# Word checks, casts, penalties, row maxima, one product and sixteen stores moved within an attention and MLP kernel on one Trainium2 core

## The chip, the cores and the metric

The kernel runs on one core of one Trainium2 chip. The time is the device time of one execution in microseconds (us). A run is reported as the median of several executions; one further execution was recorded by the hardware profiler, and all rows below come from it.

The engines are named as the trace names them: PE is the matrix engine TensorE, PEld its weight loads, DVE is VectorE, ACT is ScalarE, POOL is GpSimd, and SP is SyncE, which here only issues DMA transfers. A trailing q (ACTq, SPq) is an engine's own issuing queue. "L789" is line 789 of the kernel before.

## What is computed

A block of local attention, then a two-layer network with GELU on its result:

```python
# q, k, v: 4 batches, 8 heads, 768 positions, 64 per head
scores = scale * np.matmul(q, k.transpose(0, 1, 3, 2))
keep = is_global | is_local          # 8 global keys, 96 keys back
scores = scores - slopes[:, None, None] * dist[None, :, :]
scores = np.where(keep, scores, -1000000000.0)
a = np.exp(scores - np.max(scores, axis=-1, keepdims=True))
a = a / (np.sum(a, axis=-1, keepdims=True) + 1e-09)
x = np.matmul(a, v)                  # taken as 3072 tokens x 512
h = x @ w_in                         # 512 -> 2048
g = 0.5 * h * (1.0 + erf(h * inv_sqrt2))
return g @ w_out                     # 2048 -> 512
```

All of it is float32. The weights arrive as 8-byte words, and the kernel decodes them itself.

## The kernel before

**Tiling.** The 3072 tokens are 12 chunks of 256 rows, and the hidden width of 2048 is 8 slices of 256. One step is one slice of one chunk. `STEPS` lists the steps, and T is the number of the step in the main loop (`run`). Steps 0 and 4 to 18 do chunks 0 and 1, steps 19 to 26 do chunk 2 (the third chunk), and from step 27 on each chunk from 3 to 11 has eight steps, to step 98. A float32 operand is written as a high and a low float16 part, and each product as three float16 products (high by high, high by low, low by high). The low part is always made by a subtraction on DVE (L203, L204) from the high part, which is a cast on ACT or DVE.

**A step.** In step T the loop issues the first product `m1` of step T+1 (L702: `h` from `x` and `winh`, `winl`; 24 matmuls of 256 columns from chunk 2 on), the GELU of step T+1, and the second product `m2` of step T. `x` is the attention's result, ready for its chunk before its first step. From chunk 3 on `m2` is a seven-product scheme (`m2_seven`, L776): products P1 to P7 accumulate over the chunk's eight steps in the halves of four PSUM banks called `seven`. The left factors are quarters of the GELU (`gh`, `gl`) or sums of them (`sh`, `sl`; the sums `ss` are made at L742); the right factors are quarters of w_out (`wouth`, `woutl`) or differences of them (`sw`, made once for each slice by `sums`, L717 to L728: `sb`, `sf`, then the cast `sw` on ACT and its low part on DVE). In a chunk's last step `combine` (L789) reads the seven results out of PSUM into `u` and `o`, with which the banks come free for the next chunk. `give` stores the output rows by DMA.

**Attention.** Beside the steps the loop makes the attention of later chunks: scores `s` (L440), added penalties `pens` with a running minimum `mn` (L451), exponentials (L536), normalisation on POOL (L554), a transposition, and `av` (L604). `av` leaves PSUM as `x`, the high part by a cast on ACT (L614) and the low part on DVE (L203). Scores, `h`, `av` and transpositions share six PSUM banks.

**Checks.** Around this lie operations that serve a test at the end: `check_words` (L278, `wand`), which folds 32 pieces of reloaded weight words together; `rows` (L884, `otop`), the maxima of the output rows; and `bounds` (L208, `xtop`, `xlow`), the bounds of x.

**What sets the order.** The program is written for one loop, and a scheduler orders each engine's instructions by their dependences and by extra "behind" edges: `behind` puts an operation on DVE behind the low part of the latest GELU (`last_dve`), and `table` keeps the ACT functions that need a table in the written order. Each engine then works through its own list strictly in order.

**Names of the change.** `SUMS` tells in which step the differences of which slice are made, `PARTS` in which order the seven products of a step are issued (those of the first tuple, then the attention of slot C, then those of the second), `PENS` when the penalties of the later chunks are made (`more_pens`, then `scale_pens` in steps 14 and 15).

Of the kernel before, what the change touches and what calls it, by code (L numbers as in the profile page):

```python
# [13 lines left out]
AF = mybir.ActivationFunctionType  # L14
ALU = mybir.AluOpType
# [3 lines left out]
P = 128  # L19
# [25 lines left out]
GAP = 3  # L45
STEPS = [(c, s) for s in range(NST) for c in range(2)]
# [11 lines left out]
CAT = 2  # L58
# [4 lines left out]
GS = 2.0 ** 6  # L63
# [3 lines left out]
RATIO = 16.0  # L67
SEVEN = 3
PARTS = (("P1", "P2", "P4"), ("P6", "P7", "P5", "P3"))
ENDS = (("P6", "P7", "P5"), (("P1", "P2", "P6", "P7"), ("P4", "P5", "P3")))  # L70
SUMS = {17: 0, 18: 1, 19: 2, 21: 3, 22: 4, 25: 5, 26: 6, 29: 7}
HOME = {"P1": (0, 0), "P2": (0, 1), "P6": (1, 0), "P7": (1, 1), "P4": (2, 0), "P5": (2, 1), "P3": (3, 0)}
FACTORS = {"P1": ("A11", "B11"), "P2": ("A12", "B21"), "P3": ("S4", "B22"), "P4": ("A22", "T4"), "P5": ("S1", "T1"),
           "P6": ("S2", "T2"), "P7": ("S3", "T3")}
# [2 lines left out]
NB = NW // NG  # L77
KA = NW + 2 * NG
PENS = 13


def dap(t, off, dims):
# [23 lines left out]
def slope(h):  # L106
    return 2.0 ** (-(h + 1))


class Fast:  # L110
# [308 lines left out]
    def scale_pens(self, k):  # L419
        for i in range(4):  # L420
            h = 4 * (i // 2) + i % 2
            self.nc.gpsimd.tensor_scalar(out=self.pens2[k][:, i], in0=self.base[k], scalar1=8.0 * slope(h), scalar2=0.0,
                                         op0=ALU.mult, op1=ALU.add)

    def scores_windows(self, c, n):
        nc = self.nc
# [324 lines left out]
    def m2_seven(self, t, part):  # L751
        c, s = STEPS[t]
        if (c, s, part) == (SEVEN, 0, 0):
            self.seven = [self.ps_acc.tile([P, 2, 256], F32, name=f"seven{i}", tag="ps_acc") for i in range(2)]
            self.seven += [self.bank([P, 2, 256], f"seven{i}") for i in range(2, 4)]
        back = len(STEPS) - 1 - t
        names = PARTS[part] if back > 1 or (back, part) == (1, 0) else ENDS[0] if back else ENDS[1][part]
        for name in names:
            if (back, name) == (0, "P3"):
                self.products(t - 1, name)  # L760
            self.products(t, name)
# [47 lines left out]
    def give(self, c, k, final):  # L809
        nc, o = self.nc, self.o2[k]  # L810
        r = c * CT + k * P
        if not final or c < NCH - 1:
            args = c, k, o.rearrange("p h c -> p (h c)")
            if final:
                self.late_rows.append(args)
            else:
                self.rows(*args)
        if not final:
            return
        if c == NCH - 1:  # L820
            (nc.sync if k else nc.scalar).dma_start(self.out[r:r + P, 256:], o[:, 1])
            return
        nc.scalar.dma_start(self.out[r:r + P, :], o.rearrange("p h c -> p (h c)"))

    def gelu(self, t):
        nc = self.nc
        if STEPS[t][0] >= SEVEN:
            return self.gelu7(t)
        hp = self.h.pop(t)
        gh = self.gp.tile([P, 2, CT], F16, name=f"gh{t}", tag="gh")  # L830
        gl = self.gp.tile([P, 2, CT], F16, name=f"gl{t}", tag="gl")
        gr = self.gp.tile([P, 2, CT], F32, name=f"gr{t}", tag="gr")
        self.table(nc.scalar.activation(out=gr, in_=hp, func=AF.Gelu, scale=1.0 / (WS * XS)))
        nc.vector.tensor_scalar(out=gh, in0=gr, scalar1=GS, scalar2=None, op0=ALU.mult)
        self.last_dve = self.lo_dve(gl, gr, gh, GS).ins
        self.g[t] = (gh, gl)

# [36 lines left out]
    def send(self, c, k):  # L874
        nc, acc = self.nc, self.acc[c, k]
        o = self.sm.tile([P, DM], F32, name=f"o{c}_{k}", tag="o", bufs=3)
        r = c * CT + k * P
        scale = 1.0 / (GS * WS)
        nc.scalar.activation(out=o, in_=acc, func=AF.Copy, scale=scale)
        nc.scalar.dma_start(self.out[r:r + P, :], o)  # L880
        self.rows(c, k, o)

    def rows(self, c, k, o):
        self.behind(self.nc.vector.tensor_reduce(out=self.otop[:, c, k], in_=o.rearrange("p (h c) -> p h c", h=2),  # L884
# [38 lines left out]
    def run(self, flag_i):  # L923
# [15 lines left out]
        for self.T in range(START[0] - 1, last):  # L939
            T = self.T  # L940
# [9 lines left out]
                    self.split_weights(s, i)  # L950
            if 0 <= T - last + 9 < 6:
                self.checks(T - last + 9)
            k = T - 16 - GAP
            if 0 <= k < 64 and k % 2 == 0:
                self.check_load(k // 2)
            words = 2 <= k < 66 and k % 2 == 0
            if words and (T < 30 or T % 4 == 1):
                self.check_words((k - 2) // 2)
            if T == PENS:
                self.more_pens()  # L960
            if PENS < T < PENS + 3:
                self.scale_pens(T - PENS - 1)
            if T == 16:
                self.bounds(self.xtop, self.xlow, *(self.x[c][:, :, 0, :] for c in range(2)))
            if T in SUMS:
                self.sums(SUMS[T])
            self.turns = T >= 19
# [24 lines left out]
            if T % 8 == 3:  # L992
                for args in self.late_rows:
                    self.rows(*args)
                self.late_rows.clear()
            if words and T >= 30 and T % 4 == 3:
                self.check_words((k - 2) // 2)

    def checks(self, k):
        nc, sm = self.nc, self.const  # L1000
# [221 lines left out]
```

## Time and profile before

| what | value |
|---|---|
| median of 3 runs | 631.32 us (628.44 to 632.48) |
| the profiled execution | 629.22 us |
| its span, first to last instruction | 627.4 us |
| PE busy in the span | 599.5 us (96%) |
| DVE busy | 498.1 us (79%) |
| ACT busy | 352.9 us (56%) |
| POOL busy | 91.0 us (14%) |
| mean granted clock of PE | 0.992 |

The profiled execution took 1.8 us more than its span, which is what lies ahead of the first and behind the last instruction. In a row of the timeline, the first number is the start in us from the beginning of the span, the second the duration; neighbouring equal instructions are put together, with their number behind an x. A bracket tells how long the engine had stood idle just before, and what it waited for.

### The profile page before, as it was taken

The page shows a single profiled execution, that of the slowest core. Times are in us where ns is not written, and L with a number is a line of the kernel's source. Part 1 is how long each engine was busy: PE and PEld are TensorE (multiplying, and loading weights), DVE is VectorE, ACT ScalarE, POOL GpSimd, SP SyncE. Part 2 cuts the span into 40 slices and gives each one's busy share as a digit, 9 for nine tenths or more (in the row PEclk, how much of TensorE's full clock was granted, in tenths as well). Part 3 has the DMA queues.
Part 4 walks back from the last instruction along what each step waited for, and adds up shares of the span by engine and source line. Part 5 has one row for each costly group of instructions (what it writes and reads, how often), then busy time and mean ns, then how long its engine had stood idle before and what let it go on. Part 6 is the DMA issues. An engine that isn't in the chain of part 4 may idle for free.

```text
span 627.4 us, 19513 instructions
## 1 busy us (share of the span) xinstructions
PE 599.5 (96%) x7968; PEld 464.8 (74%) x7968; DVE 498.1 (79%) x1579; ACT 352.9 (56%) x855; POOL 91.0 (14%) x188
## 2 busy tenths in 40 slices
PE   8988999999999899999999899999999999999995
PEld 5665544445676678888888788888888888888884
DVE  7979999998788786876876776876876876875885
ACT  3777577755526566466466366366466466463331
POOL 1000006253033022022022021021021021010000
PEclk9988999999999999999999999999999999999998
DMA  9948925434371284184184175164275173100001
GB/s 272 270 173 255 261 97 202 121 66 146 114 192 57 86 218 137 37 218 136 37 218 137 36 186 159 46 159 129 104 169 180 44 195 93 37 1 2 36 1 40
DMA packets 111809, 79.47 MB, mean 127 GB/s; under 512 B 54752, under 2 KB 99296, under 8 KB 111712
## 3 DMA queue, kind: packets, MB, share of 16 engines
q1 hardware_dynamic: 107120, 70.80, 39.7%
q10 hardware_dynamic: 4592, 7.34, 3.3%
q8 instruction: 65, 1.06, 0.7%
q14 instruction: 32, 0.26, 0.1%
HBM read 71.83 MB, written 6.29 MB: 125 GB/s over the span
## 4 chain that ended last, share of the span: by engine, by line
PE 63%; DVE 23%; ACT 8%; issue 3%; POOL 2%; DMA 1%; DVEq 0%; ACTq 0%; POOLq 0%
PE h L702 26%; PE seven L776 22%; PE av L604 5%; ACT n L536 4%; PE s L440 4%; DVE gl L204 2%; DVE ss L742 2%; PE acc L863 2%; POOL n L554 2%; DVE wb L249 1%; DVE wb L251 1%; PE warm_ps L520 1%; DVE o L789 1%; DVE sl L204 1%; DVE u L789 1%
## 5 line engine op out<-in xcount | busy, mean ns | idle before, releaser
L702 PE MATMUL h<-x,winh 128*128 128x256 f16 x1344 | 227.7, 274 | 4.4 <-DVE x L203 2.9
L702 PE MATMUL h<-x,winl 128*128 128x256 f16 x672 | 184.3, 274 | 0.0
L702 PEld LDWEIGHTS <-winh 128*128 128x128 f16 x1344 | 130.3, 98 | 25.0 <-issue 4.0
L554 POOL TENSOR_SCALAR n<-n,su 128x160 f32<-128x160 f32 (+1 forms) x160 | 81.1, 527 | 450.0 <-DVE su L548 286.3
L737 ACT ACTIVATE gr<-h 128x512 f32<-128x512 f32 x72 | 43.0, 597 | 109.2 <-PE h L702 96.3
L742 DVE TENSOR_TENSOR ss<-gr 128x128 f32<-128x128 f32 x144 | 35.2, 285 | 64.6 <-ACT gr L737 64.6
L744 ACT ACTIVATE sh<-ss 128x512 f16<-128x512 f32 x72 | 45.4, 630 | 66.4 <-DVE ss L742 66.4
L776 PE MATMUL seven<-sw,sh 128*128 128x256 f16 x432 | 75.0, 273 | 1.3 <-issue 1.3
L702 PEld LDWEIGHTS <-winl 128*128 128x128 f16 x672 | 66.1, 98 | 9.1 <-issue 1.2
L776 PEld LDWEIGHTS <-sh 128*128 128x128 f16 x576 | 55.0, 98 | 8.3 <-issue 1.5
L536 ACT ACTIVATE n<-n,mn 128x160 f32<-128x160 f32 x144 | 59.5, 414 | 2.7 <-DVE mn L451 2.5
L776 PE MATMUL seven<-sw,sl 128*128 128x256 f16 x216 | 58.9, 273 | 1.2 <-DVE sl L204 1.1
L204 DVE SCALAR_TENSOR_TENSOR gl<-gr,gh 128x384 f16<-128x384 f32 (+1 forms) x96 | 57.1, 594 | 0.7
L204 DVE SCALAR_TENSOR_TENSOR sl<-ss,sh 128x512 f16<-128x512 f32 x72 | 49.6, 689 | 10.0 <-ACT sh L744 10.0
L776 PEld LDWEIGHTS <-gh 128*128 128x128 f16 x432 | 41.0, 98 | 11.9 <-ACT gr L737 3.8
L451 DVE CUSTOM_DVE_ANT_0 n<-s,pens 128x160 f32<-128x160 f32 x144 | 38.0, 320 | 3.8 <-PE s L440 2.5
L743 ACT ACTIVATE gh<-gr 128x384 f16<-128x384 f32 x72 | 37.6, 523 | 3.9 <-ACT gr L737 1.8
L776 PE MATMUL seven<-wouth,gh 128*128 128x256 f16 x144 | 39.4, 274 | 0.0
L776 PE MATMUL seven<-wouth,gl 128*128 128x256 f16 x144 | 39.3, 273 | 0.0
L776 PE MATMUL seven<-woutl,gh 128*128 128x256 f16 x144 | 39.3, 273 | 0.0
L604 PEld LDWEIGHTS av<-ptb,vr 32*64 32x64 f32 x2304 | 31.3, 130 | 5.6 <-issue 5.3
L536 ACT ACT_TABLE_LOAD x22 | 28.2, 1283 | 12.3 <-DMA qr<-qT 6.5
(160 smaller groups left out, 1103.5 us busy)
## 6 DMA issues: line engine op xcount, KB each, us to landing
w<-w SPq DMA_DIRECT2D x32, 512.0 KB, 6.4
c<-w SPq DMA_DIRECT2D x32, 512.0 KB, 4.5
kr<-kT SPq DMA_DIRECT2D x34, 320.0 KB, 4.2
vr<-v SPq DMA_DIRECT2D x60, 112.0 KB, 2.6
qr<-qT SPq DMA_DIRECT2D x11, 512.0 KB, 4.3
out<-o ACTq DMA_DIRECT2D x22, 256.0 KB, 2.3
kr<-kT SPq DMA_DIRECT2D x84, 64.0 KB, 3.6
vr<-v SPq DMA_DIRECT2D x36, 32.0 KB, 2.7
```

Source lines behind the costliest of these rows:

```text
L204: return self.nc.vector.scalar_tensor_tensor(out=out, in0=in_, scalar=scale, in1=hi, op0=ALU.mult, op1=ALU.subtract)
L440: ins = nc.tensor.matmul(sp[hh][NG * i:NG * i + NG, u, :], lhsT=qq[hr, 2 * e + p, o:o + NG], rhs=kt[hr, 2 * e + p, j, k:k + NW], start=Tru ...
L451: ins = nc.vector.tensor_tensor_reduce(out=nn[:, 2 * hh + u], in0=sp[hh][:, u, :], in1=pens, scale=-0.125, scalar=3e38, op0=ALU.add, op1=A ...
L536: self.table(nc.scalar.activation(out=nn, in_=nn, func=AF.Exp, bias=mn[:, i:i + 1], scale=-1.0, accum_out=su[:, i:i + 1]))
L554: ins = eng.tensor_scalar(out=nn, in0=nn, scalar1=su[:, i:i + 1], scalar2=0.0, op0=ALU.mult, op1=ALU.add)
L604: ins = nc.tensor.matmul(banks[i][hh * D:(hh + 1) * D, u0 * NG:u1 * NG], lhsT=vv[rows, e, b, hh * D:(hh + 1) * D], rhs=g, start=n == 0, st ...
L702: ins = nc.tensor.matmul(hp[:, f, :], lhsT=w[:, d, fs], rhs=x[:, d, e, :], start=n == 0, stop=n == 3 * NP - 1).ins
L737: self.table(nc.scalar.activation(out=gr.rearrange("p i q -> p (i q)"), in_=hp.rearrange("p f q -> p (f q)"), func=AF.Gelu, scale=1.0 / (W ...
L742: self.last_sum = nc.vector.tensor_tensor(out=ss[:, o], in0=x, in1=y, op=op).ins
L743: nc.scalar.activation(out=gh, in_=gr[:, 1:], func=AF.Copy, scale=GS)
L744: self.last_table = nc.scalar.activation(out=sh, in_=ss, func=AF.Copy, scale=GS).ins
L776: ins = nc.tensor.matmul(out, lhsT=g, rhs=w, start=s == 0 and name in ("P1", "P4", "P6", "P3") and i == 0, stop=s >= NST - 4 and i == 2, s ...
```

## The change

Six things are moved. The word checks run in steps 33 to 89 instead of 21 to 83. In chunk 2 the cast `gh` of the GELU goes from DVE to ACT (8 casts), and the eight scalings in `scale_pens` go from POOL to ACT. Four of the eight `sums` get another step. The row maxima of chunks 1 and 2 are put off until the end of the next step with T%8 == 3. In the first step of each chunk from 3 on, P6 and P4 change places. The 16 output stores of `give` for chunks 3 to 10 are issued by SP instead of ACT.

```diff
 PARTS = (("P1", "P2", "P4"), ("P6", "P7", "P5", "P3"))
+OPENS = (("P1", "P2", "P6"), ("P7", "P4", "P5", "P3"))
-SUMS = {17: 0, 18: 1, 19: 2, 21: 3, 22: 4, 25: 5, 26: 6, 29: 7}
+SUMS = {17: 0, 18: 1, 21: 2, 22: 3, 23: 4, 25: 5, 26: 6, 30: 7}
+WORDS = [T for T in range(33, 90) if T % 2 or T in (62, 70, 78)]
...
             h = 4 * (i // 2) + i % 2
-            self.nc.gpsimd.tensor_scalar(out=self.pens2[k][:, i], in0=self.base[k], scalar1=8.0 * slope(h), scalar2=0.0,
-                                         op0=ALU.mult, op1=ALU.add)
+            self.nc.scalar.activation(out=self.pens2[k][:, i], in_=self.base[k], func=AF.Copy, scale=8.0 * slope(h))
...
-        names = PARTS[part] if back > 1 or (back, part) == (1, 0) else ENDS[0] if back else ENDS[1][part]
+        names = OPENS[part] if s == 0 else PARTS[part] if back > 1 or (back, part) == (1, 0) else ENDS[0] if back else ENDS[1][part]
...
-        nc.scalar.dma_start(self.out[r:r + P, :], o.rearrange("p h c -> p (h c)"))
+        nc.sync.dma_start(self.out[r:r + P, :], o.rearrange("p h c -> p (h c)"))
...
-        nc.vector.tensor_scalar(out=gh, in0=gr, scalar1=GS, scalar2=None, op0=ALU.mult)
+        if STEPS[t][0] < CAT:
+            nc.vector.tensor_scalar(out=gh, in0=gr, scalar1=GS, scalar2=None, op0=ALU.mult)
+        else:
+            self.last_table = nc.scalar.activation(out=gh, in_=gr, func=AF.Copy, scale=GS).ins
...
         nc.scalar.dma_start(self.out[r:r + P, :], o)
-        self.rows(c, k, o)
+        if c:
+            self.late_rows.append((c, k, o))
+        else:
+            self.rows(c, k, o)
...
-            k = T - 16 - GAP
-            if 0 <= k < 64 and k % 2 == 0:
-                self.check_load(k // 2)
-            words = 2 <= k < 66 and k % 2 == 0
-            if words and (T < 30 or T % 4 == 1):
-                self.check_words((k - 2) // 2)
+            if T + 2 in WORDS:
+                self.check_load(WORDS.index(T + 2))
+            if T in WORDS and T % 4 == 1:
+                self.check_words(WORDS.index(T))
...
-            if words and T >= 30 and T % 4 == 3:
-                self.check_words((k - 2) // 2)
+            if T in WORDS and T % 4 > 1:
+                self.check_words(WORDS.index(T))
```

ACT around the GELU of step 17, the kernel before (`gr` is a GELU's result, `pt` a copy of transposed weights of the attention, `n` the scores, `sw` the cast of w_out's differences):

```order
L833 ACTIVATE gr_1670<-h_1649 128x512
L581 COPY pt_4_1660<-t_5_1674 128x384
L833 ACTIVATE gr_1714<-h_1693 128x512
L581 COPY pt_6_1704<-t_6_1700 128x384
L581 COPY pt_6_1704<-t_7_1718 128x384
L536 ACT_TABLE_LOAD
L536 ACTIVATE n_0_1743,su_0_1724<-n_0_1743,mn_0_1723 128x160 x4
L536 ACTIVATE n_1_1780,su_1_1761<-n_1_1780,mn_1_1760 128x160 x4
L833 ACT_TABLE_LOAD
L833 ACTIVATE gr_1831<-h_1816 128x512
L727 CAST sw_329<-sf_1808 128x1024
```

The same place of ACT in the changed kernel:

```order
L834 ACTIVATE gr_1670<-h_1649 128x512
L582 COPY pt_4_1660<-t_5_1674 128x384
L424 ACTIVATE pens<-rb 128x640 x4
L424 ACTIVATE pens_1451<-rb 128x320 x4
L834 ACTIVATE gr_1714<-h_1693 128x512
L582 COPY pt_6_1704<-t_6_1700 128x384
L582 COPY pt_6_1704<-t_7_1718 128x384
L537 ACT_TABLE_LOAD
L537 ACTIVATE n_0_1743,su_0_1724<-n_0_1743,mn_0_1723 128x160 x4
L728 CAST sw_329<-sf_1808 128x1024
L834 ACT_TABLE_LOAD
L834 ACTIVATE gr_1831<-h_1816 128x512
```

The eight scalings of the penalties now stand ahead of step 17's GELU (`gr_1714`), and the cast `sw` of slice 0 ahead of the table load and the GELU of step 18 (`gr_1831`).

DVE at steps 27 and 28, the kernel before (`gl_2685` and `sl_2688` belong to step 27, `ss_2749` to `sl_2751` to step 28, `x` is the low part of chunk 4's attention):

```order
L204 SCALAR_TENSOR_TENSOR gl_2685<-gr_2683,gh_2684 128x384
L725 TENSOR_TENSOR sf_2649<-sb_2648,sf_2649 128x256
L204 SCALAR_TENSOR_TENSOR sl_2688<-ss_2686,sh_2687 128x512
L884 TENSOR_REDUCE otop<-o_0_2704 128x2
L884 TENSOR_REDUCE otop<-o_1_2714 128x2
L278 SCALAR_TENSOR_TENSOR wand<-c_3_2578,wand 128x512
L203 TENSOR_TENSOR sw_1246<-sf_2649,sw_1246 128x1024
L742 TENSOR_TENSOR ss_2749<-gr_2746 128x128 x2
L742 TENSOR_TENSOR ss_2749<-gr_2746,ss_2749 128x128
L204 SCALAR_TENSOR_TENSOR gl_2748<-gr_2746,gh_2747 128x384
L204 SCALAR_TENSOR_TENSOR sl_2751<-ss_2749,sh_2750 128x512
L203 TENSOR_TENSOR x<-av_0_0_2774,x 128x128
```

The same place of DVE in the changed kernel:

```order
L206 SCALAR_TENSOR_TENSOR gl_2674<-gr_2672,gh_2673 128x384
L205 TENSOR_TENSOR sw_1246<-sf_2638,sw_1246 128x1024
L206 SCALAR_TENSOR_TENSOR sl_2677<-ss_2675,sh_2676 128x512
L743 TENSOR_TENSOR ss_2733<-gr_2730 128x128 x2
L743 TENSOR_TENSOR ss_2733<-gr_2730,ss_2733 128x128
L206 SCALAR_TENSOR_TENSOR gl_2732<-gr_2730,gh_2731 128x384
L206 SCALAR_TENSOR_TENSOR sl_2735<-ss_2733,sh_2734 128x512
L205 TENSOR_TENSOR x<-av_0_0_2758,x 128x128
L891 TENSOR_REDUCE otop<-o_0_2693 128x2
```

The word check is gone from here, the two row maxima stand behind x's low parts, and the low part of `sw` (slice 6) stands ahead of step 27's `sl` instead of behind it.

PE in step 27, the first of chunk 3, at the third product of its first tuple, the kernel before:

```order
L776 MATMUL seven_2761<-woutl_328,gh_2684 128x256
L776 LDWEIGHTS gl_2685
L776 MATMUL seven_2761<-wouth_327,gl_2685 128x256
L776 LDWEIGHTS gh_2684
L776 MATMUL seven_2763<-sw_329,gh_2684 128x256
L776 MATMUL seven_2763<-sw_329,gl_2685 128x256
```

The same place of PE in the changed kernel:

```order
L777 MATMUL seven_2745<-woutl_328,gh_2673 128x256
L777 LDWEIGHTS gl_2674
L777 MATMUL seven_2745<-wouth_327,gl_2674 128x256
L777 LDWEIGHTS sh_2676
L777 MATMUL seven_2746<-sw_329,sh_2676 128x256
L777 MATMUL seven_2746<-sw_329,sl_2677 128x256
```

The third product now reads the sums `sh` and `sl` instead of `gh` and `gl`, and writes another bank.

## Rows read from the trace of the kernel before

**Rows 1.** Busy time in a stretch: PE, PEld, DVE, ACT, POOL, then PE's clock

```profile
252.00:300.00 48.00, 47.64 (x757) 41.03 (x756) 37.01 (x126) 27.48 (x69) 6.33 (x16) 1.00 0.46 128
```

**Rows 2.** Timeline of PE where chunk 4 begins

```profile
256.07 0.27 PE L776 MATMUL seven<-woutl,gh 128*128 128x256 f16 x1
256.18 0.27 PE L776 MATMUL seven<-wouth,gl 128*128 128x256 f16 x1
256.81 0.38 PE L776 MATMUL seven<-sw,gh 128*128 128x256 f16 x2 [0.36 <-DVE u L789]
```

**Rows 3.** Waits by engine and line: us in total, times, longest

```profile
ACT gr L737 <- DVE u L789: 12.8, 7, 1.8
...
PE seven L776 <- DVE u L789: 2.5, 7, 0.4
```

**Rows 4.** Timeline of DVE just ahead of that place

```profile
254.74 0.42 DVE L789 SCALAR_TENSOR_TENSOR u<-seven,u 128x256 f32<-128x256 f32 x1
255.08 0.69 DVE L204 SCALAR_TENSOR_TENSOR sl<-ss,sh 128x512 f16<-128x512 f32 x1
```

**Rows 5.** Timeline of PE: its idle times from 149 to 229 us

```profile
149.99 0.27 PE L702 MATMUL h<-x,winh 128*128 128x256 f16 x1 [0.38 <-DVE x L203]
...
154.67 0.39 PE L863 MATMUL acc<-wouth,gh 128*128 128x512 f16 x1 [0.80 <-DVE gh L834]
...
155.46 0.39 PE L863 MATMUL acc<-wouth,gl 128*128 128x512 f16 x1 [0.19 <-DVE gl L204]
...
163.91 0.51 PE L440 MATMUL s<-kr,qr 64*32 64x160 f32 x16 [1.26 <-DVE x L203]
...
212.06 0.38 PE L702 MATMUL h<-x,winh 128*128 128x256 f16 x2 [2.29 <-DVE x L203]
...
228.80 0.28 PE L776 MATMUL seven<-sw,sl 128*128 128x256 f16 x1 [1.10 <-DVE sl L204]
```

**Rows 6.** Timeline of ACT and DVE ahead of the idle time at 163.91

```profile
161.35 1.04 ACT L727 CAST sw<-sf 128x1024 f16<-128x1024 f32 x1 [4.72 <-DVE sf L725]
162.43 1.22 DVE L203 TENSOR_TENSOR sw<-sf,sw 128x1024 f16<-128x1024 f32 x1 [1.11 <-ACT sw L727]
163.57 0.68 DVE L203 TENSOR_TENSOR x<-av,x 128x128 f16<-128x128 f32 x3
```

**Rows 7.** Timeline of DVE ahead of the idle time at 212.06

```profile
206.47 1.27 DVE L884 TENSOR_REDUCE otop<-o 128x2 f32<-128x512 f32 x2
207.66 0.68 DVE L278 SCALAR_TENSOR_TENSOR wand<-c,wand 128x512 int32<-128x512 int32 x1
208.26 1.22 DVE L203 TENSOR_TENSOR sw<-sf,sw 128x1024 f16<-128x1024 f32 x1
...
211.72 0.88 DVE L203 TENSOR_TENSOR x<-av,x 128x128 f16<-128x128 f32 x4
```

**Rows 8.** Timeline of DVE ahead of the idle time at 228.80

```profile
226.75 1.39 DVE L203 TENSOR_TENSOR sw<-sf,sw 128x1024 f16<-128x1024 f32 x1 [0.32 <-ACT sw L727]
```

**Rows 9.** Timeline of POOL: the eight scalings of the penalties

```profile
132.13 6.60 POOL L422 TENSOR_SCALAR pens<-rb 128x640 bf16<-128x640 f32 x8 [2.08 <-DVE rb L416]
```

**Rows 10.** Timeline of ACT: the GELUs of steps 17 and 18

```profile
131.47 0.60 ACT L833 ACTIVATE gr<-h 128x512 f32<-128x512 f32 x1 [2.70 <-DVE gl L204]
...
142.57 0.60 ACT L833 ACTIVATE gr<-h 128x512 f32<-128x512 f32 x1
```

**Rows 11.** Timeline of PE: step 17's last scores, step 20's first product

```profile
137.40 0.78 PE L440 MATMUL s<-kr,qr 64*32 64x160 f32 x32
...
145.32 0.38 PE L702 MATMUL h<-x,winh 128*128 128x256 f16 x2
```

**Rows 12.** Instructions by line and shape: busy us, mean ns, idle before

```profile
L834 DVE TENSOR_SCALAR gh<-gr 128x512 f16<-128x512 f32 x24 | 11.0, 459 | 5.1 <-ACT gr L833 5.1
...
L744 ACT ACTIVATE sh<-ss 128x512 f16<-128x512 f32 x72 | 45.4, 630 | 66.4 <-DVE ss L742 66.4
```

**Rows 13.** Waits of SP's own queue

```profile
SPq L315 <- PE s L440: 140.3, 8, 22.3
```

## The prediction

> **What bounds the kernel now.** I read the busy times by stretch first, then PE's timeline for each gap, then the timelines of the engine that the gap's bracket names. In a steady stretch PE is busy 47.64 of 48.00 us at full clock, DVE only 37.01 [rows 1]. So only what PE waits for counts, and the other engines have slack except where they hold PE up. Those places are few. How a gap is measured: 256-column matmuls start 0.11 apart (256.07, 256.18), so the next was due at 256.29 and came at 256.81: 0.52 lost, with 0.36 shown as idle [rows 2]. A shown idle time thus stands for about 0.16 more.
>
> The first kind of gap lies at the seven places where one chunk follows another from chunk 3 on. The waits view has it as PE waiting for DVE's u, seven times, 2.5 us in all [rows 3], so 7 x 0.52 = 3.64 us with the 0.16 each. The first tuple's third product, P4, must write a bank that DVE still reads.
>
> The second kind is single: six idle times between 149 and 229 us [rows 5]. With 0.16 on each they are 0.54, 0.96, 0.35 and 1.42 (chunk 2's steps), 2.45 and 1.26 (chunk 3's first), 6.98 in all; three more small ones of 0.1 to 0.15 I leave out. Everything that the change can win lies in these 10.6 us.
>
> **The change part by part.**
>
> *P6 for P4.* P6 writes the half whose old content DVE reads with the u at 254.74, finished at 255.16; its sl is made at 255.08 and finished at 255.77 [rows 4]. PE reaches the third product's sl matmul two matmuls after 256.29, at about 256.5. So P6 finds everything there, with 0.73 to spare. P4 now stands behind P6, the attention's av of slot C and P7: six matmuls of 0.11 and the av, so it is due 0.65 and more after 256.29, later than the 256.81 at which its bank was free. The whole 3.64 goes. In the order, step 27 shows the exchange as announced. **-3.64.** The cover is those 0.73 us: an sl later than that costs its excess seven times.
>
> *ACT in steps 17 to 20.* Here the change removes and adds. On POOL the penalties ran 6.60 us from 132.13, as soon as DVE's rb was there [rows 9]; no bracket on PE named them. Now they stand on ACT ahead of step 17's GELU, which before began at 131.47 [rows 10]. No row has such an instruction on ACT. Two casts give the slope: 1.04 us for 1024 columns [rows 6] and 0.630 for 512 [rows 12], so 0.81 ns a column and 0.215 at the start. For 640 columns that is 0.73, for 320 it is 0.47, together 4 x 1.20 = 4.8; if the start overlaps, in proportion to columns alone, 3.9. I take the middle, 4.4. The GELU then ends at 132.1 + 4.4 + 0.6 = 137.1, five late. Behind it wait the scores of step 17 (a PSUM bank that this GELU frees). Before, they were issued between the second product's matmuls, the last at 137.40 [rows 11]; now they stand behind them all, and without the scores' own time between them (about 1.0) these are over at about 136.4. PE waits about **+0.7**. From below this is 0 (if the penalties take 3.9 or less), from above all 4.4.
>
> The chain runs on: two copies, a table load, the exponentials, and now also the cast sw of slice 0 ahead of step 18's GELU. Before, this GELU ended at 143.17 [rows 10]; I walk it to about 147.2: 5 us late at step 17, some of it won back because ACT waited for DVE there, and the cast's 1.04 put ahead. Step 20's first product, at 145.32 before [rows 11], needs its bank, and PE has about 1.3 us of other work ahead of it: **+0.65** (0 to 2). The low parts of x follow at about 151.7, for which I put **+1.15** in the place of the 0.54 at 149.99.
>
> In step 19 the cast gh moves to ACT. The gap of 0.96 was a wait for gh on DVE behind the sw low part [rows 5]; it becomes a wait for gh on ACT behind a sw cast, 1.04 [rows 6], about **+1.2**, and the gl behind it **+0.3** where it was 0.35. In the other seven steps of chunk 2 gl has slack, and the 0.630 on ACT for 0.459 on DVE [rows 12] is hidden: 0.
>
> The 1.42 at 163.91 goes: x's low part stood behind a sw cast of 1.04 and the sw low part of 1.22 [rows 6], which are slice 2's and are made two steps later now. Sum of this stage: 0.7 + 0.65 + 1.15 + 1.2 + 0.3 = 4.0 added, 0.54 + 0.96 + 0.35 + 1.42 = 3.27 and about 0.25 of the small gaps removed: **+0.5**, bounds -2.5 (nothing new shows but the gh) and +4.5.
>
> The Trainium skill, "ScalarE: Activation LUTs", section "Rules for kernel authors", would have multiplications on VectorE, not on ScalarE; the rows agree in direction (0.459 against 0.630 [rows 12]), and eight casts would be worth +1.4 if each were on PE's path, of which I count none but step 19's. The same page, section "What ACT_TABLE_LOAD costs", puts an ACTIVATE with immediates at 186 ns + 0.833 ns a column, 93 ns of it overlapped; an estimate from it for the eight penalties is 4.0, by which the first wait would be 0.3 instead of 0.7.
>
> *DVE at steps 27 and 28.* The 2.45 at 212.06 comes from x's low part at 211.72, which frees a bank for h. Ahead of it stand two row maxima (1.27 together), a check (0.68) and a sw low part (1.22) [rows 7]: from 206.47 to 209.4. In the new order the check is elsewhere, the maxima come behind x, and the sw low part stands ahead of step 27's sl. x's low part comes 2 to 2.9 earlier, and PE got there at 209.6. The gap goes. But step 27's P6 now needs sl in the first tuple, and sl has the sw low part ahead of it: its end moves from 206.5 to 207.6, where PE would come at about 206.8: +0.85 (0 to 1.2). Together **-1.6**, bounds -2.45 and -0.4.
>
> *Steps 30 and 31.* The 1.26 at 228.80 waited for sl behind the sw low part of slice 7 at 226.75, 1.39 long [rows 8]. That is made one step later now, and stands ahead of step 31's gl instead, which has less cover by one product: +0.4 for -1.26, so **-0.9** (-1.26 to +0.3).
>
> *The rest.* The 32 checks take the same time elsewhere. In steps 33 to 89 DVE has 11 of 48 us idle [rows 1], and a check of 0.68 behind the low parts delays nothing that PE waits for: 0 (to +1). Stores on SP instead of ACT: ACT's GELU waits 12.8 us in all for u behind those issues [rows 3], but nothing on PE is named there, 0. On SP the stores stand ahead of later loads. SP's loads wait 140.3 us for the scores to free their buffers [rows 13], up to 22.3 each, so it has time, and a chunk's loads are issued well ahead of its scores: 0.
>
> **Sum.** -3.64 + 0.5 - 1.6 - 0.9 = -5.6, on the profiled execution's 629.22: 623.6. That execution lay 1.2 below the mean of the four executions known (630.4), and the median of three lies above both. I predict **624.8** as the time of a usual execution.
>
> **Rivals.**
>
> (a) *The middle stage gives back what it wins.* ACT becomes the engine that steps 17 to 20 wait for: penalties 4.4, a cast of 1.04 ahead of a table load, gh casts of 0.63, all in one strict list. If the GELU of step 18 is as late as the whole 4.4, the stage costs +3 instead of +0.5. For it: all the new waits hang on one chain. Against: PE has other work there (the first products of chunk 2). Then 629.22 - 3.64 + 3 - 2.5 + 1.2 = 627.3. Chance 0.30.
>
> (b) *The penalties are hidden.* PE's list has enough left at step 17, step 27's P6 waits for nothing: -3.64 - 2 - 2.45 - 1.26 = -9.3, so 621.1. For it: the scheduler has put step 16's whole second product ahead of the scores. Against: ACT's list has 4.4 us more in a place where it was never idle for as long. Chance 0.17.
>
> (c) *Slower: P6 waits for sl at each chunk's beginning.* If DVE takes the five adds u and o (0.42 each, 2.1 us) ahead of sl, sl ends at 257.9, P6 waits 1.4 instead of P4's 0.52, and 7 x 0.88 = +6.2 replaces -3.64: 629.22 + 6.2 - 2.0 + 1.2 = 634.6. It decides from a wait of 0.81, where 7 x 0.29 eats the 2.0 of the other places. For it: P6 needs sums and two casts more than P4. Against: DVE's list has sl between the adds, at 255.08 [rows 4], and the new list keeps it there. Chance 0.05.
>
> (d) *The exchange does not do what it says:* another half of the same bank is still unread, and P6 waits for the same read as P4 did. Then only the other places count: 629.22 - 2.0 + 1.2 = 628.4. For it: the trace shows only P4's wait. Against: the u at 254.74 is over 1.1 ahead. Chance 0.06.
>
> **How the numbers follow.** My forecast has 0.42, (a) 0.30, (b) 0.17, (c) 0.05, (d) 0.06. Its own bounds (-2.5 to +2 on the middle stage and the two places behind) give 622 to 627.5; with (b) below and (a) and (d) above, the range is **619.5 to 630.0**. It leaves out (c) and the tail of (b). A measurement of this kernel tells about 1% from no change, 6.3 us, since its own runs spread by 4; faster by over 1% means below 625.0, on which the forecast sits. Half of the forecast, (b) and a little of (a) are faster: 0.21 + 0.17 + 0.06 = 0.44. Slower over 1% is (c) with a part of ACT's upper bound: 0.07. Within 1%: 0.49.
>
> **What would show it.** Right: at the seven chunk beginnings no PE gap, and no PE wait for u in the waits view; no gap at 212; a GELU of step 17 that ends near 137 with PE waiting for it under 1 us; a gh on ACT that PE waits for in step 19 alone. Wrong: a PE wait for sl at the chunk beginnings ((c)); one for ACT of several us between 136 and 152 ((a)); no PE wait at all for ACT there ((b)).

## The result and the profile after

The changed kernel takes 623.18 us (median of 7 runs, 621.3 to 625.92), the kernel before 630.22 (7 runs, 626.6 to 632.48). The ratio is 0.9891, with a 95% interval from 0.9853 to 0.9928: 6.9 us less, between 4.5 and 9.3. Forecast were 624.8 and a change of -5.6.

The profiled execution of the changed kernel took 625.92 us, the longest of its seven; its span of 624.1 is only 3.3 below that of the kernel before (627.4). So the two profiles are compared by stretches, from the start of one step's GELU on ACT (L737 and L833 before, L738 and L834 after) to that of another. Where nothing random falls into a stretch, it repeats within about 0.1 us from kernel to kernel. Such a mark is ACT's: where ACT itself starts a GELU late, the mark moves without any loss on PE.

| from the GELU of step to that of step | before | after | change | forecast |
|---|---|---|---|---|
| 16 to 27 (last of chunks 0 and 1, chunk 2) | 72.63 | 72.61 | -0.02 | +0.5 |
| 27 to 29 (chunk 3 begins) | 14.45 | 13.28 | -1.17 | -1.6 |
| 29 to 33 | 24.61 | 24.37 | -0.24 | -0.9 |
| 33 to 36 | 17.36 | 16.36 | -1.00 | |
| 76 to 84 (one chunk, undisturbed) | 46.87 | 46.31 | -0.56 | -0.52 |
| 84 to 98 | 73.71 | 74.18 | +0.47 | |
| 44 to 60 (two chunks) | 96.97 | 97.84 | +0.87 | |

The seven chunk beginnings together give -3.9 (a first -1.00, six chunks of -0.56, and +0.47 at the end), where -3.64 was forecast. The -1.00 and the +0.47 belong together: before, a store holds up the GELUs of steps 36, 44 and so on to 84, so the row 33 to 36 ends with a late mark and the row 84 to 98 begins with one. With the first three rows this is -5.3, inside the measured interval of -4.5 to -9.3. The last row has -1.1 of the change in it and is +0.87 all the same: in it stand PE's waits of kind "issue", of another length in every profile (last section).

The rows of the changed kernel that answer to [rows 2, 3 and 4]. PE's timeline where chunk 4 begins:

```profile
254.99 0.27 PE L777 MATMUL seven<-wouth,gl 128*128 128x256 f16 x1
255.10 0.38 PE L777 MATMUL seven<-sw,sh 128*128 128x256 f16 x2
255.31 0.27 PE L777 MATMUL seven<-sw,sl 128*128 128x256 f16 x1
```

DVE's timeline there:

```profile
253.59 0.42 DVE L790 SCALAR_TENSOR_TENSOR u<-seven,u 128x256 f32<-128x256 f32 x1
253.93 0.69 DVE L206 SCALAR_TENSOR_TENSOR sl<-ss,sh 128x512 f16<-128x512 f32 x1
254.52 0.76 DVE L790 SCALAR_TENSOR_TENSOR o<-seven,u 128x256 f32<-128x256 f32 x2
```

P6 starts 0.11 after the matmul ahead of it; its sl was ready at 254.62, 0.69 before PE's first use of it at 255.31 (0.73 was forecast). No wait of PE for u is left in the waits view, and ACT's GELU no longer waits for u either. That wait is now SP's, whose loads behind the stores still come in time: from 125 us on no wait of PE names a load. The waits of SP's queue:

```profile
SPq L824 <- DVE u L790: 110.2, 8, 38.3
SPq L317 <- PE s L441: 81.9, 8, 25.6
```

The busy time of the stretch of [rows 1] has PE without a gap:

```profile
252.00:300.00 48.00, 48.00 (x761) 41.40 (x760) 37.46 (x129) 27.80 (x69) 6.33 (x16) 1.00 0.45 128
```

PE's timeline from 146 to 236 us, its idle times of 0.2 us and more, which answer to [rows 5]:

```profile
147.38 0.38 PE L703 MATMUL h<-x,winh 128*128 128x256 f16 x2 [1.17 <-ACT gr L834]
...
151.82 0.27 PE L703 MATMUL h<-x,winh 128*128 128x256 f16 x1 [0.82 <-DVE x L205]
...
156.73 0.39 PE L867 MATMUL acc<-wouth,gh 128*128 128x512 f16 x1 [1.03 <-ACT gh L838]
...
206.87 0.39 PE L777 MATMUL seven<-sw,sh 128*128 128x256 f16 x2 [0.41 <-ACT sh L745]
...
207.71 0.28 PE L777 MATMUL seven<-sw,sl 128*128 128x256 f16 x1 [0.46 <-DVE sl L206]
...
230.68 0.28 PE L777 MATMUL seven<-wouth,gl 128*128 128x256 f16 x1 [0.22 <-DVE gl L206]
...
235.47 0.38 PE L703 MATMUL h<-x,winh 128*128 128x256 f16 x2 [0.29 <-DVE x L205]
```

The old waits of 1.26, 2.29 and 1.10 are gone, that of 0.80 for gh on DVE too, and new ones have come: for step 18's GELU (1.33 lost with the 0.16 of the prediction), for the cast gh of step 19 (1.20) and, at step 27, for sh and sl (0.57 and 0.62). The chain that makes the first, on ACT, answering to [rows 9 and 10]:

```profile
132.31 4.05 ACT L424 ACTIVATE pens<-rb 128x640 bf16<-128x640 f32 x8 [3.30 <-DVE rb L418]
136.28 0.57 ACT L834 ACTIVATE gr<-h 128x512 f32<-128x512 f32 x1
...
144.37 1.05 ACT L728 CAST sw<-sf 128x1024 f16<-128x1024 f32 x1 [1.26 <-DVE sf L726]
145.44 1.28 ACT L834 ACT_TABLE_LOAD   x1
146.73 0.60 ACT L834 ACTIVATE gr<-h 128x512 f32<-128x512 f32 x1
```

The penalties take 4.05, step 17's GELU ends at 136.85 and step 18's at 147.33 (forecast 4.4, 137.1 and 147.2).

### The profile page after: what moved, and what is told of

It is laid out like the page before. It is cut to its first block, busy times and chain, and to the rows that moved or that the text cites. A ratio compares the mean times of both kernels' runs of the same rounds, so it can differ in the third digit from the quotient of the medians.

```text
span 624.1 us, 19510 instructions
## 1 busy us (share of the span) xinstructions
PE 597.6 (96%) x7968; PEld 464.5 (74%) x7968; DVE 493.2 (79%) x1571; ACT 360.8 (58%) x871; POOL 80.4 (13%) x180
## 4 chain that ended last, share of the span: by engine, by line
PE 72%; DVE 13%; ACT 8%; issue 2%; DMA 2%; POOL 1%; SPq 0%; DVEq 0%; ACTq 0%; POOLq 0%
PE h L703 31%; PE seven L777 25%; PE av L605 5%; PE s L441 4%; ACT n L537 3%; PE acc L867 3%; DVE wb L251 2%; DVE wb L253 1%; PE acc L852 1%; DVE gl L206 1%; DMA kr<-kT 1%; DVE n L503 1%; DVE wb L248 1%; PE h L697 1%; POOL n L555 1%
## 5 line engine op out<-in xcount | busy, mean ns | idle before, releaser
L555 POOL TENSOR_SCALAR n<-n,su 128x160 f32<-128x160 f32 (+1 forms) x160 | 76.9, 503 | 460.1 <-DVE su L549 395.3
L738 ACT ACTIVATE gr<-h 128x512 f32<-128x512 f32 x72 | 43.0, 597 | 103.4 <-PE h L703 103.3
```

What stands on the lines that cost most here:

```text
L555: ins = eng.tensor_scalar(out=nn, in0=nn, scalar1=su[:, i:i + 1], scalar2=0.0, op0=ALU.mult, op1=ALU.add)
L738: self.table(nc.scalar.activation(out=gr.rearrange("p i q -> p (i q)"), in_=hp.rearrange("p f q -> p (f q)"), func=AF.Gelu, scale=1.0 / (W ...
```

## The experiments

The stretches show where the time went, not which of the edits did it (there are seven, with the moved `sums`). The first runs undo one edit at a time, or make one alone.

### The exchange alone

The kernel before with:

```diff
+OPENS = (("P1", "P2", "P6"), ("P7", "P4", "P5", "P3"))
...
-        names = PARTS[part] if back > 1 or (back, part) == (1, 0) else ENDS[0] if back else ENDS[1][part]
+        names = OPENS[part] if s == 0 else PARTS[part] if back > 1 or (back, part) == (1, 0) else ENDS[0] if back else ENDS[1][part]
```

> The kernel before with one edit: P6 for P4 in each chunk's first step. My theory (the exchange alone removes PE's wait for u, everything else of the change is another matter): the seven gaps of 0.52 disappear, a steady chunk takes 46.3 us instead of 46.87, and the time falls by 3.6 to 3.9 us, a ratio of 0.994. Rival 1 (the exchange needs the stores off ACT, whose GELU waits behind their issue for 1.8 us at each boundary): sl is late without them, PE waits for sl instead, the chunk stays above 46.7 and the time falls by less than 1. Rival 2 (the exchange is worth the whole measured gain): the time falls by 7.

Measured: 627.78 us, ratio 0.9967 (0.9946 to 0.9989). The undisturbed chunk (steps 76 to 84) takes 46.86, as before. So the exchange alone wins nothing at the chunks' beginnings, and what the median shows (some 2 us) is in none of the first stretches: 16 to 27 takes 72.61, 27 to 29 14.46, 29 to 33 24.60. In its one profile 1.5 us lie ahead of step 16's GELU, at 126.27 where it was at 127.79, and there the edit changes nothing. Rival 1 is right in its cause and wrong in its place, and the median fell by more than its 1. PE's timeline where chunk 4 begins (the view ends within the last row):

```profile
254.75 0.38 PE L777 MATMUL seven<-sw,sh 128*128 128x256 f16 x2
254.97 0.27 PE L777 MATMUL seven<-sw,sl 128*128 128x256 f16 x1
255.17 0.46 PE L605 MATMUL av<-ptb,vr 32*64 32x128 f32 x12
255.95 0.48 PE L605 MATMUL av<-ptb,vr 32*64 32x128 f32 x16 [0.32 <-ACT gr L738]
```

P6 goes through without a wait, sl included; 0.6 us behind it av waits for ACT's gr, and 0.58 is lost there instead of 0.52. The waits view shows it seven times, with what gr waits for:

```profile
ACT gr L738 <- DVE u L790: 12.8, 7, 1.8
...
PE av L605 <- ACT gr L738: 2.2, 7, 0.3
```

and ACT's timeline shows why:

```profile
254.92 0.34 ACTq L824 DMA_DIRECT2D out<-o  x1
255.30 0.60 ACT L738 ACTIVATE gr<-h 128x512 f32<-128x512 f32 x1 [1.82 <-DVE u L790]
255.78 0.34 ACTq L824 DMA_DIRECT2D out<-o  x1
```

The store stands ahead of the GELU in ACT's list and waits for DVE's o, which is made on the same line as u. The GELU waits with it, though its h is there, and av, which by the code shares its PSUM banks with h, waits for the GELU.

### Without the exchange

The changed kernel with `OPENS` not used (the old line of `names`).

> The changed kernel with P4 back in its place. My theory: the seven gaps of 0.52 come back, a chunk takes 46.87 again, and the time is 3.6 to 3.9 above the changed kernel, that is 3 below the kernel before (ratio to it 0.995); in step 27 the two PE waits for sh and sl (0.57 and 0.62) go, so that chunk 3 gains about 1.1 of it back at most. Rival (the rest of the change is worth nothing): the time equals that of the kernel before within 1 us.

Measured: 626.64, ratio to the kernel before 0.9939 (0.9906 to 0.9972). The waits view has the old row again:

```profile
PE seven L777 <- DVE u L790: 2.5, 7, 0.4
```

The chunk takes 46.75, 0.12 less than before. The stores on SP alone were not run; if the word checks, which also moved in these chunks, count for nothing there, 0.12 is what the stores win without the exchange. Steps 27 to 29 take 12.46 instead of 13.28: the exchange costs 0.82 where chunk 3 begins. The two waits of step 27 (0.57 and 0.62) are gone, and one of 0.51 for x's low part has come. The theory holds.

### The penalties on POOL

The changed kernel with `scale_pens` as before:

```diff
-            self.nc.scalar.activation(out=self.pens2[k][:, i], in_=self.base[k], func=AF.Copy, scale=8.0 * slope(h))
+            self.nc.gpsimd.tensor_scalar(out=self.pens2[k][:, i], in0=self.base[k], scalar1=8.0 * slope(h), scalar2=0.0, op0=ALU.mult, op1=ALU.add)
```

> The changed kernel with the eight scalings of the penalties back on POOL. My theory (ACT's strict list, made 4 us later by them, is what PE waits for at step 20's first product): the GELU of step 18 comes back from 146.7 to about 142.6, PE's wait of 1.33 for it goes and the wait of 0.99 for x's low part shrinks to about 0.5; the stretch from the GELU of step 16 to that of step 26, 68.9 in the changed kernel, becomes 66.9 to 67.6, and the time is 1.3 to 2 lower than that of the changed kernel. Rival 1 (later waits take up what is won, since PE only comes earlier to a gh that is set by DVE's differences): 68.5 or more, under 0.4 gained. Rival 2 (POOL's instructions slow DVE while they run, and that is what moving them won): 69.5 or more, slower.

Measured: 620.08, ratio 0.9848 (0.9814 to 0.9883). Steps 16 to 27 take 70.43 instead of 72.61, 2.18 less, all of it in steps 16 to 22 (42.39 for 44.58); the expectation named the stretch to step 26, which takes 66.70 instead of 68.88. ACT's timeline, and the two idle times of PE that are left:

```profile
142.37 0.60 ACT L834 ACTIVATE gr<-h 128x512 f32<-128x512 f32 x1
143.85 1.05 ACT L728 CAST sw<-sf 128x1024 f16<-128x1024 f32 x1 [0.89 <-DVE sf L726]
```

```profile
149.80 0.27 PE L703 MATMUL h<-x,winh 128*128 128x256 f16 x1 [0.39 <-DVE x L205]
154.03 0.39 PE L867 MATMUL acc<-wouth,gh 128*128 128x512 f16 x1 [0.36 <-ACT gh L838]
```

The wait for step 18's GELU is gone, the one for x is 0.55 instead of 0.99, and the one for gh 0.53 instead of 1.20. My theory held, with a little more than I had put on it (the median lies 3.1 lower, where the stretch gives 2.2); the penalties on ACT are the largest loss in the change.

### The casts gh on DVE

The changed kernel with chunk 2's casts on DVE again.

> The changed kernel with chunk 2's eight casts gh back on DVE. My theory (of the eight only step 19's is waited for, and on DVE it would stand behind the low part of sw as before): the wait of 1.20 before step 19's second product stays within 0.4 of that, no other appears, the stretch from step 16's to step 26's GELU stays at 68.9 within 0.5, the time the same within 0.5. Rival (a cast costs more on ACT than on DVE, and all eight count): 1.4 lower. Second rival (DVE is what holds up x's low parts in chunk 2, and the cast's going freed it): 1 to 2 higher, with a gap before the scores of step 20 as in the kernel before.

Measured: 625.2, ratio 0.9917 (0.9888 to 0.9946); steps 16 to 27 take 74.69, 2.08 more than the changed kernel. My theory falls, and the second rival is near in its size, though not in its place: no gap comes back at the scores of step 20. PE's timeline in step 19:

```profile
156.93 0.39 PE L864 MATMUL acc<-wouth,gh 128*128 128x512 f16 x1 [1.47 <-DVE gh L835]
...
157.87 0.39 PE L864 MATMUL acc<-wouth,gl 128*128 128x512 f16 x1 [0.33 <-DVE gl L206]
...
158.92 2.79 PE L605 MATMUL av<-ptb,vr 32*64 32x128 f32 x128
```

The two waits are 0.64 longer together than those of the changed kernel (1.63 + 0.49 for 1.20 + 0.28). Behind them, after 2 us in which PE was busy for 0.74, its granted clock falls to 0.50, the lower of its two levels (1.2 instead of 2.4 GHz). The windows of that kernel, 2 us each, the clock in the third column from the right:

```profile
156.00:158.00 2.00, 0.74 (x3) 0.23 (x4) 2.00 (x5) 0.26 (x1) 0.00 (x0) 1.00 0.01 2
158.00:160.00 2.00, 2.00 (x52) 1.27 (x51) 1.60 (x3) 0.60 (x1) 0.00 (x0) 0.67 0.04 13
160.00:162.00 2.00, 2.00 (x105) 1.70 (x90) 0.12 (x1) 0.41 (x3) 0.00 (x0) 0.50 0.34 126
```

The same 128 matmuls of av take 1.80 us in the changed kernel and 2.79 here: with the 0.64 this makes 1.63 of the 2.08, and the products on either side of av, at the same low clock, take 0.3 more. So about a third of the 2.08 is waiting, and most of the rest is the clock, for which one profile alone is the witness. That the casts bring the clock down in other executions too isn't shown.

### The stores back on ACT

The changed kernel with `nc.scalar.dma_start` in `give`.

> The changed kernel with the 16 stores of give back on ACT's queue. After the run of the exchange alone, my theory is that the exchange and the stores only win together: a store on ACT's queue waits for DVE's o, the GELU behind it is late, the bank of its h stays taken, and av in the first step waits for that bank. Then the chunk's period goes back from 46.31 to 46.87, with a gap of 0.58 in av at each of the seven places, and the time is 3.9 higher than that of the changed kernel. Rival, my prediction's own view (a store on ACT costs nothing on PE): the period stays at 46.31 and the time the same within 0.5.

Measured: 626.36, ratio 0.9928 (0.9901 to 0.9955), 3.2 above the changed kernel. The undisturbed chunk takes 46.89, and the wait is where it was expected, 0.66 lost at chunk 4 and 0.61 or 0.62 at the others (the view ends within the row):

```profile
256.48 0.77 PE L605 MATMUL av<-ptb,vr 32*64 32x128 f32 x38 [0.40 <-ACT gr L738]
```

### Exchange and stores, and nothing else

The kernel before with the exchange and with `nc.sync.dma_start` in `give`.

> The kernel before with two edits, P6 for P4 in each chunk's first step and the stores of give on SP. My theory (the two together are the whole of the gain at the chunks' beginnings, and need nothing else of the change): the period is 46.31, no gap at the seven places, the time 3.9 lower than before (ratio 0.994). Rival (checks, sums or row maxima of the change are needed as well, since DVE's u and o hold the banks): the period stays above 46.6 and the time falls by less than 2.

Measured: 623.45, ratio 0.9892 (0.985 to 0.9934), the same as the whole change. The undisturbed chunk takes 46.31, and in the waits view no row of PE at seven or av names u or gr. So the two edits together are the whole gain at the chunks' beginnings, and need nothing else. The steps before are those of the kernel before: 72.70, 14.46, 24.59. By the stretches the rest of the change is worth 1.5 here (14.46 - 13.28 and 24.59 - 24.37 and 0.09), by the medians 0.3; the difference is below what these runs tell.

### Row maxima and checks in their old places

The changed kernel with `rows` in `send` for all chunks, and the changed kernel with the old steps of the checks.

> The changed kernel with the row maxima of chunks 1 and 2 in their old place. My theory (they stood ahead of x's low part of chunk 4, whose margin to PE is only 0.1 us in the changed kernel): the two maxima, 1.19 us, come back ahead of step 28's sums, a gap of 1.0 to 1.2 appears before the first product at about 211, and the stretch from step 27's to step 29's GELU is 14.3 to 14.5 instead of 13.28. Rival (the check and the sw low part made the gap of 2.45, and the maxima find room): under 0.3 more.

> The changed kernel with the word checks in their old steps. My theory (one check of 0.60 comes back ahead of step 28's sums, where the margin is 0.1): a gap of 0.3 to 0.6 before the first product at about 211, the stretch from step 27's to step 29's GELU 13.6 to 13.9; nothing elsewhere, since DVE has idle time in later steps. Rival (checks are free in both places): 13.28 within 0.1.

Measured, one run each: steps 27 to 29 take 13.66 with the old rows, 0.38 more, between theory and rival; 0.30 is lost before the first product at 211.48. With the old checks they take 13.31, the same as in the changed kernel, though PE waits where the theory had it:

```profile
210.19 0.38 PE L703 MATMUL h<-x,winh 128*128 128x256 f16 x2 [0.71 <-DVE x L205]
```

The 0.87 lost here is given back by step 27's P6, which waits 0.27 instead of 0.57 + 0.62. The reason is in DVE's timeline of that kernel: with the check back, the scheduler has put the low part of `sw` behind step 27's `sl` again, as in the kernel before, so that this run puts back two things.

```profile
205.20 0.68 DVE L206 SCALAR_TENSOR_TENSOR sl<-ss,sh 128x512 f16<-128x512 f32 x1
205.80 0.68 DVE L280 SCALAR_TENSOR_TENSOR wand<-c,wand 128x512 int32<-128x512 int32 x1
206.40 1.22 DVE L205 TENSOR_TENSOR sw<-sf,sw 128x1024 f16<-128x1024 f32 x1
```

In sum the checks are free in both places, as the rival said. Neither of the two runs brings back the 2.45 of before. The kernel with the exchange and the stores alone, in which all three operations stand where they were, loses 2.06 at this place.

### Three versions that go on from there

The kernel with the penalties on POOL, and then: the exchange only in chunks after the first of the scheme; besides, the differences of slice 7 in step 32; or instead in step 29, their old place. A fourth run is the changed kernel with all differences in their old steps.

```diff
-        names = OPENS[part] if s == 0 else
+        names = OPENS[part] if s == 0 and c > SEVEN else
-SUMS = {17: 0, 18: 1, 21: 2, 22: 3, 23: 4, 25: 5, 26: 6, 30: 7}
+SUMS = {17: 0, 18: 1, 21: 2, 22: 3, 23: 4, 25: 5, 26: 6, 29: 7}
```

> The changed kernel with the penalties back on POOL, and with P4 in its old place in chunk 3's first step alone (before it no chunk of this scheme has filled the banks, so nothing waits for u there). My theory (the waits of 0.6 for sh and 0.6 for sl in step 27 are the exchange's own): the stretch from step 27's to step 29's GELU falls from 13.33 to 12.5, the time 0.8 below that of the kernel with the penalties on POOL alone, 619.3. Rival (PE only comes earlier to the first product behind it, whose bank x's low part frees with a margin of 0.1): the 0.8 becomes a wait there, 13.2 or more.

> The same, with the differences of slice 7 made in step 32 instead of 30. My theory (the three waits of 0.39, 0.35 and 0.45 at 228 to 233, in step 31, hang on the differences' subtractions and sw low part among that step's gl and sl): they go, the stretch from step 29's to step 33's GELU falls from 24.37 to 23.2 to 23.5, the time another 1 lower, 618.3. Rival (the differences come into the way of another step, as when they went from step 29 to 30): 24.1 or more, or a new wait for sw in step 33 or 34.

> The changed kernel with the differences of all slices in their old steps. My theory (the move took the sw of slice 2 out of the way of x's low part in step 20, but the move of slice 7 by one step won little): the wait of about 1.4 before the scores of step 20 comes back, the stretch from step 16's to step 22's GELU is 45.5 to 46.5 instead of 44.58, the one from step 29's to step 33's stays within 0.4 of 24.37. Rival (the differences had slack with the casts on ACT): both the same within 0.2.

> The kernel of run e9 (penalties on POOL, P4 in its old place in chunk 3's first step) with the differences of slice 7 made in step 29 again, the other slices as in the change. My theory (with checks and row maxima out of the way, step 29 has room for them, and their move to step 30 cost what the kernel with all old steps won): the stretch from step 29's to step 33's GELU falls from 24.36 to 23.7, the time 0.6 below e9's 619.3, which a few runs can hardly tell; the stretch decides. Rival (the gain needs the other slices' old steps as well): 24.3 or more.

| version | median us | ratio (interval) | 16 to 27 | 27 to 29 | 29 to 33 |
|---|---|---|---|---|---|
| penalties on POOL | 620.08 | 0.9848 (0.9814 to 0.9883) | 70.43 | 13.33 | 24.37 |
| and P4 first in chunk 3 (e9) | 619.26 | 0.9822 (0.9796 to 0.9848) | 70.36 | 12.46 | 24.36 |
| and slice 7 in step 32 (e10) | 619.19 | 0.9841 (0.9806 to 0.9875) | 70.35 | 12.42 | 25.10 |
| and slice 7 in step 29 (e12) | 619.34 | 0.9829 (0.9803 to 0.9855) | 70.35 | 12.46 | 23.71 |
| changed kernel, all old steps of the differences (e11) | 621.57, one run | | 72.81 | 13.37 | 23.71 |

The first does what was expected of it, 0.87 less in its stretch. The second fails: the differences at step 32 come into the way of the next chunk's scores, and PE waits for the penalties' addition on DVE:

```profile
237.14 0.39 PE L703 MATMUL h<-x,winh 128*128 128x256 f16 x2 [1.51 <-DVE mn L452]
```

This wait and a later one lie behind step 33, so the table shows too little of them: from step 29's to step 44's GELU this kernel takes 88.45, e9 87.07. That the median is no worse than e9's goes with 1.5 us that its profile wins ahead of step 16, where the two kernels are the same.

The third wins 0.65 in its stretch, as expected; its median does not show so little. The one with all old steps shows the same 23.71, so that moving slice 7 to step 30 was a loss of 0.66. It did not show the 1.4 at the scores of step 20 that I expected: steps 16 to 22 take 45.01 for 44.58, steps 16 to 27 only 0.20 more, and no such wait is there. It is not there either with the casts on DVE and the new steps. So it isn't shown which edit took it away: in both kernels the penalties are on ACT and waits stand ahead of it. With the casts on ACT the move of slice 2 was worth little.

All three versions are below both kernels; by its stretches e12 is the best, though the medians don't tell the three apart.

## Why the prediction was right

The time lay 1.6 us from the forecast, in its range, and of the listed cases the likeliest came. The size came out, but the mechanism of its largest term was half seen. By the stretches its four terms came out 0.3 and 0.5 lower and 0.4 and 0.7 higher than forecast, so that their errors nearly cancel in the sum. The rest, from -5.3 by the stretches to the measured -6.9, no run explains. Point by point:

**The gain at the chunks' beginnings** had the right size (-3.9 for -3.64) and place. Its cause was put down to one edit alone: "The whole 3.64 goes" with P6 for P4, and the stores "nothing on PE is named there, 0". These two terms fail. The exchange alone gives 46.86 a chunk, the change without the exchange 46.75, exchange and stores 46.31. I had the row in hand [rows 3], 12.8 us of ACT's GELU behind the stores, and counted it at nothing because no wait of PE named it. It was hidden by the wait for u that the other edit removes: with that gone, it was the next to end. The term came right by luck, because the change made both edits. Whoever had taken the exchange alone by this working would have forecast 3.6 us and got nothing at these places.

**ACT in steps 17 to 20** (+0.5 forecast, -0.02 measured). The walk had the penalties at 4.4 (4.05), the end of step 18's GELU at 147.2 (147.33), the wait for x at 1.15 (0.99), that for gh at 1.2 (1.20) and for gl at 0.3 (0.28). The one behind the scores of step 17, +0.7, did not come; the one for step 18's GELU was 1.33 instead of 0.65, so that their sum was right by luck (1.35 for 1.33). The removed waits went as listed. By these waits alone the stage would come out at +0.5 (3.80 added, 3.27 removed). The working had put another 0.25 to small gaps; the 0.3 that is still missing to the measured -0.02 wasn't traced. By the Trainium skill, "ScalarE: Activation LUTs", section "What ACT_TABLE_LOAD costs", the eight penalties had been estimated at 4.0, nearer to the 4.05 than my 4.4. The same page's section "Rules for kernel authors" speaks against the casts on ScalarE; one cast alone agrees, 0.630 on ACT and 0.459 on DVE [rows 12]. The kernel with the casts on DVE is nevertheless slower by 2.08 in that stretch: 0.64 of it is longer waiting for DVE in step 19, and most of the rest is PE's low clock behind it, seen in one profile.

**Steps 27 and 28** (-1.6 forecast, -1.17 measured): the gap of 2.45 went, and P6's wait in the first step came, mis-sized: 1.19 for 0.85, because PE waits for sh, then once more for sl. My reason for the gap, though, named three operations as if their times added up. Of the two that were put back by themselves, the maxima give 0.38 and the check 0.03, which had the place of `sw` change with it: a wait that grows in one place shrinks in the next.

**Steps 30 and 31** (-0.9 forecast, -0.24 measured) is the term that was mis-sized most. I took only the sl behind sw as the wait and 0.4 for gl; measured are three waits: 0.39 for gl, 0.35 at av for a GELU that stands behind the cast sw on ACT, and 0.45 for x's low part. The old step does better by 0.66.

**The rivals.** (a) has the mechanism in it (the penalties cost 2.18, shown by the run with them on POOL). The waits that went paid that back; by the run with the casts on DVE, their move to ACT has a part in it. (b), (c) and (d) did not come; (c)'s margin of 0.73 was 0.69 and held at all seven places.

## What to carry to other kernels

A wait that costs nothing may only be hidden by a longer one at the same place. Before an edit that removes a wait is counted, list what else the next instructions on that engine need, and when each is there: here the release of a bank by a GELU that stood behind a store. A store whose data come late from another engine does not belong into the list of an engine that has computing to do behind it. And where several small waits lie in a row, put one edit back at a time, see whether the order of other operations changed with it, and measure the whole stretch; the single wait that goes says little.

## What the hardware showed besides

PE waited, in every kernel's profile, for nothing that the profile shows ("issue"), at two or three of the same places: behind the GELUs of steps 48, 52 and 56. In the profile of the changed kernel:

```profile
352.62 0.38 PE L777 MATMUL seven<-sw,sh 128*128 128x256 f16 x2 [1.99 <-issue]
```

Steps 44 to 60 take 92.6 us without it (two chunks of 46.31). They took 97.84 there, 94.12 with the penalties on POOL, 94.89 with the two edits alone, 100.85 without the exchange (of 93.5). So from 1.5 to 7.4 us beyond the two chunks lie in this one place, and step 16's GELU starts anywhere from 126.0 to 128.0 us in the kernels' profiles. That would account for medians that differ by 2 us where the other stretches agree; each kernel was profiled once, so how much it changes from one execution of a kernel to the next isn't shown. Where it comes from was not tried.

After some of these waits the granted clock fell to the lower of its two levels (1.2 of 2.4 GHz), after others of the same length it did not: 0.50 from 354 to 356 us in the changed kernel's profile behind the 1.99, but 1.00 throughout behind one of 1.98 with the old row maxima, and 1.00 behind the 2.29 at 212.06 of the kernel before [rows 5].

One operation of DVE, on x's bounds, ran slower while POOL made the penalties (131.94 to 138.54 us); first the kernel with the penalties on POOL, then the changed one:

```profile
133.35 1.20 DVE L210 TENSOR_TENSOR xtop<-x 128x1024 f16<-128x1024 f16 x1
```

```profile
133.45 0.69 DVE L210 TENSOR_TENSOR xtop<-x 128x1024 f16<-128x1024 f16 x1
```

It didn't decide the time: the kernel with the slower DVE there is the faster one, by 2.18 us in that stretch.
